# Attention and a two-layer network on one core: first q and k loaded in 1 KB packets, first products in two parts, and a new planned order

## The chip, the core and the metric

The kernel runs on one core of one Trainium2 chip. The core has five engines with a queue of their own each: TensorE (PE, matrix products), VectorE (DVE), ScalarE (ACT), GpSimd (POOL) and SyncE (SP, which only issues transfers here). They meet through semaphores. The metric is the device time of one launch in microseconds (us). Three runs of the kernel before gave 601.85, 602.19 and 604.92 us, so its median is 602.19 us.

## What is computed

Four sequences of 768 tokens with 8 heads of 64 numbers. A token attends to the first `n_global` (8) tokens and to itself and the 95 before it (`n_local` = 96), with a penalty that grows with distance. The result x (3072 tokens by 512) goes through a layer of 2048 units and back. All inputs are 32 bit floats, but the weights come as 64 bit floats and the two counts as 64 bit integers.

```python
scores = q @ k.T / sqrt(64) - slope[h] * dist        # kept where global or local, else -1e9
a = softmax(scores);  x = a @ v                      # x: 3072 x 512
h = x @ w_in                                         # 512 -> 2048
g = h * sigmoid(1.702 * h)
out = g @ w_out                                      # 2048 -> 512
```

## The kernel before

**Tiles.** Tokens are worked on in 24 blocks of 128 (`n`), and in 12 chunks `c` of two blocks each. The 2048 units are cut into 8 steps `s` of 256. The first four blocks (0 to 3) are the first block of each sequence; they need keys of their own block only, so the kernel starts with them (`prep_first`, `first`). The other 20 go through `prep` and `unit`, two heads at a time: scores `s` on PE (L536), a row maximum on DVE, the exponential and a split into a large and a small 16 bit part on ACT and DVE, a transposing transfer (`pt<-hl`), and the products with the values, `pv` (L567 to L569). `finish` divides by the sums, splits x into a large part `x_hi` and a small part `x_lo` and turns it (`xT`): by PE for blocks 0 to 3, by a transposing transfer for the others.

**Products.** A 32 bit product is made of three 16 bit ones: large by large, large by small, small by large. `up` (L787) makes h for chunks 0 to 2, in two halves (`fi`) of 12 products each; `up_two` (L827, tiles `pa`, `pb`) does it for chunks 3 to 11 with fewer products; `down` and `down_two` add into `y` (L895). `weights` makes the 16 bit weights out of the 64 bit words on DVE and ACT (`w`, `wa`, lines L370 to L378).

**The first four blocks.** `prep_first` loads q and k of a block into `raw`, 128 tokens on 128 partitions; a token's 64 numbers of one head are 256 bytes in a row, and such a packet is what a transfer moves at a time. PE turns two heads at once, a 128x128 block, into `tq` (L422, four turns for q and four for k); ACT and DVE bring the turned q into `QZ` and ACT the turned k into `KF` (its tile is shown as `hl`; L429). `first` then makes the scores (L604, in 32 bit, with a mask product L605), their maximum (`top`, L609), turns that (`aux`, L612), makes the scores again the other way round (`sT`, L623 to L625), takes the exponential (`pt`, L636) and multiplies by the values (`pv`, L631). `x` is made on DVE (L665 to L669), turned on PE (`tx`, L689), its large part is copied on ACT (L692) and the small part is made on DVE (L693). The masks `mm` depend on the two counts, which a transfer on ACT's queue brings to all 128 partitions (`ci`, L244); `counts`, `own` and `other` (L308 to L332) work them out on DVE.

**Order.** Nothing is ordered by hand. `Work.order` plans: each task has a price per engine and a due time, worked back from the tasks that wait for it, and each engine takes the ready task with the earliest due time. `NUDGE` shifts the due times of named groups (`up11` is chunk 1, step 1). Before 50 us the planner puts spare products (`spare`, L1056, tile `idle`, two of 128x512) where it finds PE without work for more than 0.5 us. What the engines do is that fixed order, each waiting for semaphores. Rings of buffers (`Ring`) hold the tiles; `tq`, `h`, `pa`, `pb`, `tx` of most blocks and `idle` share a ring of two PSUM banks (`r_h`). At the end the last `y` is scaled on ACT and written, and a flag that says whether the fast path held is read (L1066).

Of the kernel before, what the change touches and what calls it, by code (L numbers as in the profile page):

```python
# [19 lines left out]
P = 128  # L20
# [9 lines left out]
NUDGE = {"T2": -1.5, "down02": 1.4, "down05": -8.2, "down07": -0.8, "down103": 6.7, "down113": -5.5,  # L30
# [9 lines left out]
FIRST = 4  # L40
SIGN = [{"DVE": 0.62, "ACT": 1.0}]
TURN_X = 4
WARM, GAP = 50.0, 0.5
# [44 lines left out]
class Work:  # L88
# [15 lines left out]
    def order(self):  # L104
# [18 lines left out]
        for t in self.tasks:  # L123
            t.due += NUDGE.get(t.tag, 0.0)
        free = dict.fromkeys(("PE", "DVE", "ACT", "POOL", "SP"), 0.0)
# [4 lines left out]
        while len(done) < len(self.tasks) + spared:  # L130
            moved = False
            for e in free:
# [21 lines left out]
                if best is None:  # L154
                    if e != "PE" or now > WARM or now < worked + (GAP if worked > 7.0 else 0.0):
                        continue
                    best = self.spare(spared)
                    b = best.bufs[0]
                    if len(b.ring.taken) >= b.ring.bufs and (b.ring.taken[-b.ring.bufs].left or b.ring.taken[-b.ring.bufs].end > now):
                        continue  # L160
                    b.users, b.left = [best], 1
                    ready[best] = now
                    spared += 1
                t, us = best, best.on[e]
# [45 lines left out]
def kernel(  # L210
# [34 lines left out]
    cf = const.tile([P, 2, 2], F32, name="cf")  # L245
# [61 lines left out]
    def counts(e):  # L307
        nc.vector.tensor_copy(cf, ci)  # L308
        nc.vector.tensor_scalar(cnt, cf[:, :, 0], 0.0, None, ALU.is_lt)
        nc.vector.tensor_add(cnt, cnt, cf[:, :, 1])  # L310
        nc.vector.scalar_tensor_tensor(cnt, cnt, float(2 ** 32), cf[:, :, 0], ALU.mult, ALU.add)
# [29 lines left out]

    wk.tag = "masks"
    m0 = add({"POOL": 2.0}, places, bufs=[ints], want=-9.0)
    m0 = add({"DVE": 1.3}, distances, [m0], [ints, flt, mk], -4.0)
    late = add({"POOL": 1.0}, lambda e: None, [m0], want=0.0)
    m0 = add({"DVE": 0.65}, counts, [m0, late])
    covers = add({"DVE": 1.2}, covered, [m0])
    covers.soon = 300.0
    m1 = add({"DVE": 1.1}, own, [m0], [flt, mk])
# [49 lines left out]

    def guard(n, raw, ld, want):  # L400
# [7 lines left out]
    def prep_first(n):  # L408
# [6 lines left out]
        ld = load(n, raw, (0, 1))  # L415
        turned = []
        for z in range(2):
            tq = Buf(r_h, [P, NU, P], F32, f"tq{n}_{z}")

            def turn(e, z=z, tq=tq):  # L420
                for u in range(NU):
                    nc.tensor.transpose(tq()[:, u], raw()[:, z, 2 * u:2 * u + 2, :].rearrange("p h d -> p (h d)"), ident)  # L422

            turned.append((tq, add({"PE": 4 * TURN}, turn, ld[z:z + 1], [raw, tq])))

        def taken(to, z, part):
            tq, t1 = turned[z]
            return add({"ACT": 0.6, "DVE": 0.7}, lambda e: (
                nc.scalar.mul(to(), tq()[part], SX) if e == "ACT" else nc.vector.tensor_scalar(to(), tq()[part], SX, None, ALU.mult)),  # L429
                [t1], [tq, KF if z else QZ])  # L430

        rows = [slice(D * z, D * z + D) for z in range(2)]
        d["qk_ready"] = [zero, *(taken(lambda z=z: QZ()[rows[z], :, z, :], 0, rows[z]) for z in range(2)), taken(KF, 1, slice(0, P))]
# [85 lines left out]
    def unit(n, u, want_s, want_v):  # L519
# [29 lines left out]
        for j in range(2):  # L549
            t2 = add({"DVE": 0.365}, lambda e, j=j: rows(e, j), [t1, M2], [sp, pr])  # L550
# [30 lines left out]
    def first(n, want):  # L581
# [15 lines left out]
        for f in range(2):  # L597
# [9 lines left out]
            t1 = add({"PE": 4 * (mm_s + MM128)}, scores, [M1[f], *d["qk_ready"]], [sp, *QKs], want + 1.2 * f)  # L607
# [43 lines left out]
    xT, x_ready = {}, {}  # L651

    def finish(n):
# [30 lines left out]
        if n < TURN_X:  # L684
# [7 lines left out]
            t3 = add({"ACT": 0.5}, lambda e: nc.scalar.copy(xT[c]()[:, 0:NCC, t, :], tx()), [t2], [tx, xT[c]])  # L692
            x_ready[n] = add({"DVE": 0.61}, lambda e: nc.vector.tensor_sub(xT[c]()[:, NCC:, t, :], tx(), xT[c]()[:, 0:NCC, t, :]),  # L693
# [84 lines left out]
    def up(c, s, want):  # L778
# [11 lines left out]
        def hh():  # L790
            return ph().rearrange("p f t -> p (f t)")

        t1 = ups[c, s] = [add({"PE": 12 * MM256}, lambda e, fi=fi: mms(e, fi), [x_ready[2 * c], x_ready[2 * c + 1], W_ready[s, 0]],
                  [ph, xT[c], WT[s, 0]], want + 1.3 * fi) for fi in range(2)]
# [258 lines left out]
    def spare(n):  # L1053

        z = Buf(r_h, [P, 4 * P], F32, f"idle{n}")
        return Task({"PE": 2 * MM512 * (2 if n < 5 else 1)}, lambda e: [nc.tensor.matmul(z(), idle[:, 0:P], idle, start=True, stop=True)  # L1056
                                                  for _ in range(2)], (), [z], 0.0)
# [209 lines left out]
```

## Time and profile before

| what | value |
|---|---|
| median of three runs | 602.19 us |
| the profiled execution's own time | 602.55 us |
| its span in the profile | 600.8 us |
| busy: PE, DVE, ACT | 587.3, 502.9, 471.6 us |
| spare products (L1056) | 26 |

A span begins with the first instruction and ends with the last, and 1.75 us of the profiled execution's time lie around it. A row of the timeline gives start, duration, engine, line, tile, shape and count, and in brackets how long the engine was idle before it and what ended that. A PE record of a product lasts longer than the product holds up the next one: consecutive products overlap, so what one costs is read from one start to the next.

### The profile page before, as it was taken

The numbers are of one execution on the slowest core, as the hardware profiler recorded it, in microseconds if no ns is written. First come the engines' busy times: TensorE is split into PE (matmuls) and PEld (weight loads), VectorE is DVE, ScalarE is ACT, GpSimd is POOL, SyncE is SP. The second block draws the span as 40 slices with busy tenths as digits, with TensorE's granted clock in tenths as the row PEclk, the third lists the DMA queues.
The fourth block names the chain that finished last, engine by engine and source line by source line (L and its number), as shares of the span: only waits on it lengthen the run. The fifth ranks groups of instructions, "written<-read, shape, count | busy, mean of one in ns | idle before, by whom it ended". The sixth has DMA issues, their size and how long they took to land.

```text
span 600.8 us, 17038 instructions
## 1 busy us (share of the span) xinstructions
PE 587.3 (98%) x6816; PEld 445.8 (74%) x6816; DVE 502.9 (84%) x1177; ACT 471.6 (78%) x1098; POOL 5.8 (1%) x18
## 2 busy tenths in 40 slices
PE   8989999999999999999999999999999999999995
PEld 5878767776777867777677777777678778867895
DVE  6998999999999999789699789798979978766532
ACT  3878899978758988888688899788989988844432
POOL 3000000000000000000000000000000000000000
PEclk9999999999999999999999999999999999999998
DMA  8998898999976778969996999999989999910001
GB/s 221 316 249 254 235 251 191 196 187 203 198 139 127 160 117 182 199 141 206 194 222 153 227 204 233 206 229 198 240 181 227 227 205 237 231 29 3 36 2 40
DMA packets 268502, 109.58 MB, mean 182 GB/s; under 512 B 249536, under 2 KB 250048, under 8 KB 268416
## 3 DMA queue, kind: packets, MB, share of 16 engines
q1 hardware_dynamic: 268128, 108.43, 85.7%
q8 instruction: 55, 0.90, 0.6%
q14 instruction: 31, 0.25, 0.1%
q10 hardware_dynamic: 288, 0.00, 0.0%
HBM read 57.67 MB, written 6.29 MB: 106 GB/s over the span
## 4 chain that ended last, share of the span: by engine, by line
PE 82%; DMA 7%; ACT 4%; DVE 4%; issue 1%; SPq 1%; DVEq 0%; ACTq 0%
PE y L895 35%; PE pa L827 13%; PE h L787 10%; PE pb L827 10%; PE s L536 4%; DMA pt<-hl 2%; DMA out_dram<-yo 1%; PE s L604 1%; PE pv L567 1%; PE pv L568 1%; PE pv L569 1%; PE sT L623 1%; DMA raw<-in_k_dram 1%; DMA xT<-x 1%; DMA ws_00again<-in_moe_w_in_dram 1%
## 5 line engine op out<-in xcount | busy, mean ns | idle before, releaser
L895 PE MATMUL y<-w,g 128*128 128x512 f16 (+1 forms) x1248 | 266.9, 363 | 0.0
L895 PEld LDWEIGHTS <-g 128*128 128x128 f16 x1248 | 117.9, 98 | 103.3
L827 PEld LDWEIGHTS <-w 128*128 128x128 f16 x1728 | 101.2, 98 | 4.8
L552 ACT ACTIVATE p<-p,NM 128x232 f32<-128x232 f32 x160 | 76.5, 481 | 7.3 <-DVE NM L542 7.1
L827 PEld LDWEIGHTS <-T 128*128 128x128 f16 x1296 | 77.1, 98 | 6.2 <-issue 0.2
L787 PE MATMUL h<-xT,w 128*128 128x256 f16 x576 | 69.4, 273 | 0.5 <-DMA xT<-x 0.5
L542 DVE CUSTOM_DVE_ANT_0 p<-s,mm 128x232 f32<-128x232 f32 x160 | 57.7, 396 | 8.4 <-PE s L536 7.8
L787 PEld LDWEIGHTS <-w 128*128 128x128 f16 x576 | 55.2, 98 | 9.6 <-issue 0.8
L868 DVE SCALAR_TENSOR_TENSOR g<-t,g 128x512 f16<-128x512 f32 x72 | 49.3, 688 | 12.3 <-ACT g L867 12.0
L557 DVE TENSOR_TENSOR hl<-p,hl 128x464 f16<-128x464 f32 x80 | 50.9, 637 | 8.1 <-ACT hl L556 7.9
L867 ACT ACTIVATE g<-t 128x512 f16<-128x512 f32 x72 | 45.0, 628 | 9.5 <-DVE t L860 8.1
L859 ACT ACTIVATE t<-h 128x512 f32<-128x512 f32 (+1 forms) x72 | 35.9, 516 | 18.0 <-DVE h L835 14.9
L556 ACT CAST hl<-p 128x464 f16<-128x464 f32 x80 | 46.1, 577 | 4.2 <-DMA pt<-hl 2.3
L835 DVE TENSOR_TENSOR h<-pb,h 128x256 f32<-128x256 f32 x72 | 29.5, 420 | 22.6 <-PE pb L827 19.3
L827 PE MATMUL pa<-xS,T 128*128 128x128 f16 x648 | 45.0, 219 | 0.1
L860 DVE SCALAR_TENSOR_TENSOR t<-t,h 128x512 f32<-128x512 f32 (+1 forms) x72 | 38.3, 554 | 4.8 <-ACT t L859 4.2
L536 PEld LDWEIGHTS <-QK 128*128 128x128 f16 x640 | 36.4, 98 | 4.3 <-DMA QK<-QK 0.8
L536 PE MATMUL s<-QK 128*128 128x128 f16 x320 | 38.5, 219 | 0.6 <-DMA QK<-QK 0.6
L827 PE MATMUL pb<-xS,w 128*128 128x128 f16 x540 | 37.5, 219 | 0.0
L827 PE MATMUL pa<-xT,w 128*128 128x128 f16 x540 | 37.0, 219 | 0.0
L567 PE MATMUL pv<-VR,pt 128*128 128x64 f16 x288 | 34.8, 193 | 1.3 <-DMA pt<-hl 1.3
L569 PE MATMUL pv<-VR,pt 128*128 128x64 f16 x288 | 34.9, 193 | 0.0
(181 smaller groups left out, 1080.7 us busy)
## 6 DMA issues: line engine op xcount, KB each, us to landing
ws<-in_moe_w_in_dram SPq DMA_DIRECT2D x8, 1024.0 KB
ws<-in_moe_w_out_dram SPq DMA_DIRECT2D x8, 1024.0 KB
raw<-in_q_dram SPq DMA_DIRECT2D x24, 256.0 KB
raw<-in_k_dram SPq DMA_DIRECT2D x24, 256.0 KB
out_dram<-yo SPq DMA_DIRECT2D x22, 256.0 KB
QK<-QK SPq DMA_DIRECT2D x40, 128.0 KB
raw<-in_v_dram SPq DMA_DIRECT2D x20, 256.0 KB
ws_00again<-in_moe_w_in_dram SPq DMA_DIRECT2D x8, 512.0 KB
```

The lines of the kernel that those rows point to most:

```text
L536: nc.tensor.matmul(sp()[:, j, lo:hi], d["QK"]()[:, 0, h, :], K[:, 1 + z, h, P - (hi - lo):], start=(z == 0), stop=(z == 1), skip_group_che ...
L542: nc.vector.tensor_tensor_reduce(out=pr()[:, j, :], in0=sp()[:, j, :], in1=m, scale=-1.0 / SC, scalar=3.0e38, op0=ALU.add, op1=ALU.min, ac ...
L552: ex.append(add({"ACT": 0.473}, lambda e, j=j: nc.scalar.activation(pr()[:, j, :], pr()[:, j, :], AF.Exp, bias=NM[:, n, hs[j]:hs[j] + 1], ...
L556: t4 = add({"ACT": 0.5}, lambda e: nc.scalar.copy(hl()[:, 0, :, SKIP:], pr()), ex, [pr, hl])
L557: t5 = add({"DVE": 0.55}, lambda e: nc.vector.tensor_sub(hl()[:, 1, :, SKIP:], pr(), hl()[:, 0, :, SKIP:]), [t4], [pr, hl])
L567: nc.tensor.matmul(o, ph, V[:, 0, h], start=(s == 0), stop=False, skip_group_check=True)
L569: nc.tensor.matmul(o, pl, V[:, 0, h], start=False, stop=(s == ns - 1), skip_group_check=True)
L787: nc.tensor.matmul(ph()[:, fi, :], w1(s, cc, z, fi), X[:, y, cc, :], start=(j + cc == 0), stop=(j == 2 and cc == NCC - 1))
L827: nc.tensor.matmul(o()[:, fi], w, x()[:, y * NCC + 2 * k + cc, t], start=(first and fi + j + cc == 0), stop=(last and j + cc == 3), skip_g ...
L867: t4 = add({"ACT": 0.53}, lambda e, g=g, tt=tt: nc.scalar.mul(g()[:, 0], tt(), SG / (SX * SW)), u, [tt, g])
L868: t5 = add({"DVE": 0.61}, lambda e, g=g, tt=tt: nc.vector.scalar_tensor_tensor(g()[:, 1], tt(), SG / (SX * SW), g()[:, 0], ALU.mult, ALU.s ...
L895: nc.tensor.matmul(y(), part(zg, f), w2(s, z, f % 2)[:, m], start=(begin and f + j == 0), stop=(end and j == 2 and f == 2 * len(steps) - 1 ...
```

## The change

Four things are edited, and the planner makes a new order of the whole program out of them.

- **Loads of blocks 0 to 3** (`load_pairs`): a partition holds four consecutive tokens of one head (1 KB in a row), for two heads. Each of q and k comes in two transfers, where it was one. PE therefore turns 64 columns at a time: four turns as before into partitions 0 to 63 of `tq`, and four more products with the identity, in 32 bit and not in the turning mode, into partitions 64 to 127. The evictions read `tq` in a new order of columns; for blocks 0 and 1 that of k is cut in two halves (`KHALF`), and the first scores wait for the first half only.
- **Counts**: they go to one partition and are worked out there; one small product on PE (`pc`) with a row of ones brings them to all partitions. The second group of masks (`M2`) is made of four tasks on ACT alone; it was one on DVE or ACT.
- **First step's products** (`up`, s = 0, chunks 0 and 1): all 16 products with x's large part go first and wait only for the large part; the 8 with the small part follow and wait for it.
- **Spare products**: from the sixth on, one and not two. `HOLD` is empty and its code does nothing. `NUDGE` is another table.

```diff
-NUDGE = {"T2": -1.5, "down02": 1.4, "down05": -8.2, "down07": -0.8, "down103": 6.7, "down113": -5.5,
...
+NUDGE = {"T0": 4.2, "T1": 0.1, "T3": 0.6, "down01": -3.2, "down02": -4.7, "down03": -0.9, "down06": -32.8, "down07":
...
+KHALF = 2
...
+HOLD = {}
...
-    ci = const.tile([P, 2, 2], I32, name="ci")
+    ci = const.tile([1, 2, 2], I32, name="ci")
...
-        nc.scalar.dma_start(ci[:, j], src.bitcast(I32).rearrange("(o x) -> o x", o=1).broadcast_to([P, 2]))
+        nc.scalar.dma_start(ci[:, j], src.bitcast(I32).rearrange("(o x) -> o x", o=1))
...
+    pc = Buf(r_pv, [P, 2], F32, "pc")
+    m0 = add({"PE": 0.2}, lambda e: nc.tensor.matmul(pc(), row, c1, start=True, stop=True), [m0], [pc], COUNTS)
+    m0 = add({"DVE": 0.15}, lambda e: nc.vector.tensor_copy(cnt, pc()), [m0], [pc], COUNTS)
...
-    M2 = add({"DVE": 2.3, "ACT": 2.6}, lambda e: slopes(e, slice(0, 2)), [m2], [mk])
+    M2 = [add({"ACT": 0.65}, lambda e, f=f: slopes(e, slice(0, 2), range(2 * f, 2 * f + 2)), [m2], [mk]) for f in range(4)]
...
+    def load_pairs(n, raw):
+
+        b, i = place(n)
+        ld = []
+        for z in range(2):
+            src = (q, k)[z][b, :, i * P:(i + 1) * P, :].rearrange("(u e) (j t) d -> e u j (t d)", e=2, t=4)
+            dst = raw()[:, z].rearrange("p (e t) d -> p e (t d)", e=2)
+            ld.append([add({"SP": 0.45}, lambda e, src=src, dst=dst, o=o: nc.sync.dma_start(dst[:, o], src[o]), bufs=[raw]) for o in range(2)])
+        return ld
...
-                for u in range(NU):
-                    nc.tensor.transpose(tq()[:, u], raw()[:, z, 2 * u:2 * u + 2, :].rearrange("p h d -> p (h d)"), ident)
+                for u in range(4):
+                    nc.tensor.transpose(tq()[0:D, u], raw()[:, z, u, :], ident)
+                for u in range(4):
+                    nc.tensor.matmul(tq()[D:P, u], raw()[:, z, 4 + u, :], ident, start=True, stop=True, skip_group_check=True)
...
+        if s == 0 and c < 2:
+            large = add({"PE": 16 * MM256}, lambda e: [some(e, ((0, 0), (1, 0)), fi, fi == 0, False) for fi in range(2)],
+                        [x_large[2 * c], x_large[2 * c + 1], W_ready[s, 0]], [ph, xT[c], WT[s, 0]], want)
+            t1 = [add({"PE": 8 * MM256}, lambda e: [some(e, ((0, 1),), fi, False, True) for fi in range(2)],
+                      [large, x_ready[2 * c], x_ready[2 * c + 1]], [ph, xT[c], WT[s, 0]], want + 1.8)]
...
-        return Task({"PE": 2 * MM512 * (2 if n < 5 else 1)}, lambda e: [nc.tensor.matmul(z(), idle[:, 0:P], idle, start=True, stop=True)
-                                                  for _ in range(2)], (), [z], 0.0)
+        return Task({"PE": MM512 * (4 if n < 5 else 1)}, lambda e: [nc.tensor.matmul(z(), idle[:, 0:P], idle, start=True, stop=True)
+                                                                    for _ in range(2 if n < 5 else 1)], (), [z], 0.0)
```

How the order moves is seen at three places. The first is PE's queue behind the first eight spare products, at about 5 us. `tq0_0` is block 0's turned q, `tq0_1` its k, `tq1_0` block 1's q. Before:

```order
L422 MATMUL tq0_0_140<-ident_73,raw0_107 128x128 x3
L1056 LDWEIGHTS idle_71
L1056 MATMUL idle4_146<-idle_71 128x512 [waits PE_49]
L1056 LDWEIGHTS idle_71
L1056 MATMUL idle4_146<-idle_71 128x512
L422 MATMUL tq0_1_154<-ident_73,raw0_107 128x128 [waits DMAHW3_49,PE_49]
...
L422 MATMUL tq1_0_182<-ident_73,raw1_115 128x128 [waits DMAHW4_49,PE_49]
```

Of the change, the same place:

```order
L449 MATMUL tq0_0_155<-ident_76,raw0_95 64x128 x3
L451 MATMUL tq0_0_155<-ident_76,raw0_95 64x128 [waits DMAHW3_49]
L451 MATMUL tq0_0_155<-ident_76,raw0_95 64x128 x3
L362 MATMUL pc_168<-c1_68,row_69 128x2 [waits DVE_49]
L449 MATMUL tq0_1_170<-ident_76,raw0_95 64x128 [waits DMAHW4_49,PE_49]
L449 MATMUL tq0_1_170<-ident_76,raw0_95 64x128 x3
L451 MATMUL tq0_1_170<-ident_76,raw0_95 64x128 [waits DMAHW5_49]
L451 MATMUL tq0_1_170<-ident_76,raw0_95 64x128 x3
L449 MATMUL tq1_0_190<-ident_76,raw1_96 64x128 [waits DMAHW6_49,PE_49,Activation_49]
```

The spare products between the turns are gone, each turn has four more products (L451), `pc` stands between them, and `tq1_0`, which lies in the bank of `tq0_1`, now waits for ACT, where spare products used the banks in between. Of the 26 spare products 10 are left: these first eight and two before `sT` of block 0. All five spare tasks left are among the first five, which still hold two products.

The second place is ACT's queue at the start, with the evictions of the turned q and k of blocks 0 and 1 (k goes to `hl0` and `hl1`) and the masks `mm`. Before:

```order
L429 ACTIVATE QZ0_120<-tq0_0_140 64x4x128
L429 ACTIVATE hl0_89<-tq0_1_154 128x512
L338 ACTIVATE mm_91<-mk_126 128x128 x4
L429 ACTIVATE QZ1_133<-tq1_0_182 64x4x128
L429 ACTIVATE hl1_90<-tq1_1_218 128x512
L613 CAST mT0_79<-aux0_262 8x128
```

Of the change:

```order
L460 ACTIVATE hl0_92<-tq0_1_170 128x256 [waits PE_49]
L460 ACTIVATE hl0_92<-tq0_1_170 128x256
L351 ACTIVATE mm_94<-mk_135 128x128 [waits DVE_49]
L351 ACTIVATE mm_94<-mk_135 128x128 x3
L460 ACTIVATE QZ1_152<-tq1_0_190 64x4x128 [waits DVE_49]
L460 ACTIVATE hl1_93<-tq1_1_204 128x256 [waits PE_49]
L460 ACTIVATE hl1_93<-tq1_1_204 128x256
L351 ACTIVATE mm_94<-mk_135 128x256 x8
```

Each eviction of k is two instructions of half the size, and the eight wide masks, which DVE made before, stand on ACT ahead of the first weights.

The third place is PE's queue from the end of block 1's `sT` to the first `h`, at about 25 to 33 us. Before:

```order
L631 MATMUL pv1_374<-VF1_109,pt1_0_343 128x65 x4
L689 MATMUL tx0_383<-ident_73,x0_365 128x128 x4
L631 MATMUL pv1_374<-VF1_109,pt1_1_381 128x65 x3
L631 MATMUL aux1_304<-VF1_109,pt1_1_381 128x65
L1056 LDWEIGHTS idle_71
L1056 MATMUL idle11_400<-idle_71 128x512
...
L689 MATMUL tx1_415<-ident_73,x1_408 128x128 x4
L422 MATMUL tq2_0_421<-ident_73,raw2_336 128x128 x4
L422 MATMUL tq2_1_428<-ident_73,raw2_336 128x128 x4
L1056 LDWEIGHTS idle_71
L1056 MATMUL idle12_436<-idle_71 128x512
```

Of the change:

```order
L449 MATMUL tq2_0_394<-ident_76,raw2_97 64x128 x4
L451 MATMUL tq2_0_394<-ident_76,raw2_97 64x128 x4
L726 MATMUL tx0_406<-ident_76,x0_388 128x128 x4
L668 MATMUL pv1_413<-VF1_115,pt1_0_382 128x65 x4
L668 MATMUL pv1_413<-VF1_115,pt1_1_403 128x65 x3
L668 MATMUL aux1_332<-VF1_115,pt1_1_403 128x65
L449 MATMUL tq2_1_438<-ident_76,raw2_97 64x128 x4
L451 MATMUL tq2_1_438<-ident_76,raw2_97 64x128 x4
L726 MATMUL tx1_449<-ident_76,x1_435 128x128 x4
L449 MATMUL tq3_0_457<-ident_76,raw3_98 64x128 x4
L451 MATMUL tq3_0_457<-ident_76,raw3_98 64x128 x4
```

Three of the turns of blocks 2 and 3 stand where the spare products and waits were, ahead of the first `h`; before, the two of block 3 came behind it. `tq2_1` lies in the bank of `tq2_0`, and `tq3_1`, which follows the scores of block 2, in that of the first `h`. Behind 50 us the same tasks stand in another order; for one, between the last `pv` of block 5 and the first `h` of chunk 2 there were 4 groups of `s`, 3 of `y`, 2 of `h` and one of `pv`, and there are now 4, 4, 4 and one.

More of the change, by code (lines that the diff above doesn't have):

```diff
@@ L163, in order @@
                     spared += 1
+                if e in HOLD and best.due < 1e8:
+                    soon = [at for t, at in ready.items() if e in t.on and now < at <= now + min(HOLD[e], 0.5 * best.on[e]) and
+                            t.due < best.due - 1.0 and t.early() <= at]
+                    if now < held.setdefault((best, e), max(soon, default=0.0)):
+                        continue
                 t, us = best, best.on[e]
@@ L549, in unit @@
         for j in range(2):
-            t2 = add({"DVE": 0.365}, lambda e, j=j: rows(e, j), [t1, M2], [sp, pr])
+            t2 = add({"DVE": 0.365}, lambda e, j=j: rows(e, j), [t1, *M2], [sp, pr])
             checks.append(t2)
@@ L605, in scores @@
                     nc.tensor.matmul(sp()[:, j], id16, mm[:, h, 2], start=False, stop=True, skip_group_check=True)
-            t1 = add({"PE": 4 * (mm_s + MM128)}, scores, [M1[f], *d["qk_ready"]], [sp, *QKs], want + 1.2 * f)
+            t1 = add({"PE": 4 * (mm_s + MM128)}, scores, [M1[f], *(d["first_ready"][f] if n < FIRST else d["qk_ready"])], [sp, *QKs], want + 1.2 * f)
             d.setdefault("S", []).append(t1)
```

54 lines of the change are left out of this document (38 added, 16 removed), and 10 rows, old and new, of the table NUDGE.

## The prediction

> **What bounds the kernel now.** I read the busy shares first, then PE's busy time by stage, then what PE waited for.
>
> ```profile
> PE 587.3 (98%) x6816; PEld 445.8 (74%) x6816; DVE 502.9 (84%) x1177; ACT 471.6 (78%) x1098; POOL 5.8 (1%) x18
> ...
> 25.00:30.00 5.00, 4.27 (x35) 3.58 (x35) 4.54 (x11) 5.00 (x8) 0.00 (x0) 1.00 1.15 312
> 30.00:35.00 5.00, 4.09 (x36) 3.59 (x36) 4.83 (x8) 3.31 (x4) 0.00 (x0) 1.00 0.50 188
> 35.00:40.00 5.00, 3.80 (x33) 3.05 (x31) 4.83 (x7) 4.08 (x7) 0.00 (x0) 1.00 1.08 294
> 50.00:100.00 50.00, 50.00 (x405) 36.66 (x403) 46.07 (x84) 44.31 (x70) 0.00 (x0) 1.00 0.89 226
> ```
>
> The stages' columns are the stretch, its length, then the busy times of PE, PE's weight loads, DVE, ACT and POOL. PE is the bound: behind 50 us it has no gap for long stretches, and only the first 50 us leave it short of work. So the time is PE's products, plus PE's waits, plus a start and an end that the change doesn't touch. PE's waits, longest sum first (us in total, times, longest):
>
> ```profile
> PE idle L1056 <- ACT hl L429: 1.6, 2, 0.9
> PE idle L1056 <- POOL idle L252: 1.3, 1, 1.3
> PE pv L567 <- DMA pt<-hl: 1.3, 2, 0.8
> PE tx L689 <- DVE x L669: 0.7, 1, 0.7
> PE s L536 <- DMA QK<-QK: 0.6, 1, 0.6
> PE aux L612 <- DVE top L609: 0.6, 1, 0.6
> PE tq L422 <- DVE QZ L429: 0.6, 1, 0.6
> PE h L787 <- DMA xT<-x: 0.5, 1, 0.5
> PE tq L422 <- DMA raw<-in_k_dram: 0.2, 1, 0.2
> ```
>
> Beside the 1.3 us for the very first weights, which stay, six waits lie in the first steps (1.6+0.7+0.6+0.6+0.2 = 3.7 us) and four behind them (1.3+0.6+0.5 = 2.4 us, the `pv`, `s` and `h` rows). That is all a better order can win, together with the spare products.
>
> ```profile
> 15.68 0.27 PE L612 MATMUL aux<-ident,top 128*8 128x128 f32 x1
> 15.79 0.59 PE L1056 MATMUL idle<-idle 128*128 128x512 bf16 x2
> ```
>
> One allowance: a product's record runs past the start of the next one, here 0.27 us long with the next after 0.11. Idle time counts from the record's end, so each wait costs 0.16 us more than it shows: the six early ones 3.7+1.0 = **4.7 us**, the four later ones 2.4+0.6 = **3.0 us**.
>
> **The change part by part.** I sum against the profiled execution's own time, 602.55 us (span 600.8 and 1.75 around it), which is 0.36 over the median of 602.19.
>
> *Turning q and k.*
>
> ```profile
> 1.33 3.59 PE L1056 MATMUL idle<-idle 128*128 128x512 bf16 x8 [1.33 <-POOL idle L252]
> 4.74 1.09 PE L422 MATMUL tq<-ident,raw 128*128 128x128 f32 x4
> 5.61 1.06 PE L1056 MATMUL idle<-idle 128*128 128x512 bf16 x2
> 6.84 0.77 PE L422 MATMUL tq<-ident,raw 128*128 128x128 f32 x4 [0.17 <-DMA raw<-in_k_dram]
> 8.30 1.02 PE L1056 MATMUL idle<-idle 128*128 128x512 bf16 x4 [0.68 <-ACT hl L429]
> 9.16 0.60 PE L422 MATMUL tq<-ident,raw 128*128 128x128 f32 x4
> 9.59 0.59 PE L1056 MATMUL idle<-idle 128*128 128x512 bf16 x2
> 10.03 0.38 PE L604 MATMUL s<-hl,QZ 128*128 128x128 f32 x2
> 10.25 0.22 PE L605 MATMUL s<-mm,id 128*128 128x128 bf16 x1
> 10.30 0.44 PE L604 MATMUL s<-hl,QZ 128*128 128x128 f32 x2
> 10.58 0.22 PE L605 MATMUL s<-mm,id 128*128 128x128 bf16 x1
> ...
> 25.03 1.00 PE L631 MATMUL pv<-VF,pt 128*128 128x65 f32 x8
> 25.87 0.61 PE L689 MATMUL tx<-ident,x 128*128 128x128 f32 x4
> ```
>
> Four turns take 9.59 - 9.16 = 0.43 us, 0.11 each; their number stays, 32. A 32 bit product in two passes takes 10.25 - 10.03 = 0.22 us. The 32 new products with the identity have this shape but for 64 columns of weights, which no row shows at that width. Bounds: 0.21 us, from `pv` (8 passes in 25.87 - 25.03 = 0.84), and 0.28, the second score product (10.30 to 10.58). I take 0.22, the one that follows 32 bit work as these will: 32 x 0.22 = **+7.0 us** (6.7 to 9.0). All of it lies on PE, which has nothing to hide it beyond waits and spare products. `pc` adds 0.1.
>
> *Spare products.* Sixteen of 26 go. At 8.30 four take 9.16 - 8.30 = 0.86, 0.215 each; the two at 5.61, like the first eight ((4.74 - 1.33)/8 = 0.43), ran at half that speed. 14 x 0.215 + 2 x 0.43 = **-3.9 us**. That later spare tasks hold one product changes nothing: none is planned beyond the fifth.
>
> *Half speed at the start.* The clock column says 1.00 all along, yet products take twice as long until about 7.2 us (0.43 against 0.215). The first four turns have that in both kernels; the four products behind them, now at 5.6 us, get it too: 8 passes x 0.11 = **+0.8 us** (0 to 1.5).
>
> *Early waits.* The six, 4.7 us, go with their places: the turns and `pv` that fill them are the added work. New ones I work out from the order. `tq1_0` waits for both halves of `hl0`:
>
> ```profile
> 7.65 0.60 ACT L429 ACTIVATE hl<-tq 128x512 f32<-128x512 f32 x1 [1.20 <-PE tq L422]
> 9.24 0.91 ACT L338 ACTIVATE mm<-mk 128x128 bf16<-128x128 f32 x4 [0.99 <-DVE mk L327]
> ...
> L843 ACT COPY h<-pa 128x256 f32<-128x256 f32 x36 | 13.1, 364 | 10.1 <-PE pa L827 9.9
> ```
>
> PE ends `tq0_0` at 4.74+0.87+1.7 = 7.3 and `tq0_1` at 8.7; ACT starts 0.2 later and needs two pieces of 0.36 (the group with 256 columns), to 9.6: 0.9 us for PE. At 30 us `tq2_1` waits for the second half of block 2's `QZ`, which stands behind a weight step on ACT, and `tq3_1` for the DVE step that frees h's bank; I put them at 0.8 and 0.5, about the longest waits of that kind there now (0.9 for ACT, 0.6 for DVE in the rows of waits). Together **+2.2 us** (0 to 4.5, the lower end if ACT and DVE run ahead, the upper about the early waits of before).
>
> *The 1 KB packets and the counts.* q's four turns follow the eight spare products without a gap (4.74), so q came in time and its earlier landing wins nothing; k's wins the 0.2 us counted above. The counts reach one partition, and their four DVE steps now stand ahead of the first `QZ`. ACT had its first masks done at 9.24+0.91 = 10.2; with `tq0_0` ready 1.5 us later (7.3 for 4.74+1.09) they come by 11.7 at most, and PE, at 9.6 + 2 x 1.3 for block 1's turns, reaches the first scores at 12.2. So neither is late, by half a us; beyond that each us of slip would be a us. The evictions read PSUM with a stride, which no row shows: I take their old durations, 0.6 us; nothing less is likely, twice as long would add about 0.4 us to the wait of `tq1_0`. The eight masks moved to ACT (8 x 0.36 = 2.9 us) lie beside 16 score products of 0.33 each (0.28 to the start of the mask product, at 10.58, and 0.05 for that), 5.3 us of PE. The first `h` starts without the small part, but at 33 us it comes behind five further turns, by when DVE, on my count, has that part too: nothing (down to -0.6, the one DVE step that it skips).
>
> Sum of the first steps: 7.0 + 0.1 - 3.9 + 0.8 - 4.7 + 2.2 = **+1.5 us**.
>
> *The order behind 50 us.* The products are the same, so only waits count. Transfers took:
>
> ```profile
> 126.37 1.31 PE h L787 x12
> 128.03 0.41 PE s L536 x8
> 128.44 1.29 PE y L895 x6
> 131.96 4.97 DMA xT<-x
> 289.29 6.21 DMA pt<-hl
> 344.08 4.54 DMA QK<-QK
> 403.17 6.29 DMA pt<-hl
> 410.03 0.67 PE pa L827 x12
> ```
>
> For `xT` PE had 4 groups of `s`, 3 of `y`, 2 of `h` and a `pv` (0.35) to do meanwhile, 1.6+3.9+2.6+0.35 = 8.5 us; now 4, 4, 4 and one, 12.4. For the first `pv` of block 14 (289 us): 6 groups of `pa`/`pb`, 2 of `y`, 3 of `s`, 7.8 us; now 7, 4 and 2, 10.7. For that of block 19 (403 us): 4, 4, 2, 8.7; now 7, 4, 3, 11.1. These three waits were 0.5+1.3 and 3 x 0.16, 2.3 us, and each gets over twice what it lacked, so I drop them. The one for `QK` (0.8) I keep, and 0.6 for one new wait of that size, since every group has moved. **-1.7 us** (-3.0, all gone, to +2.0, two or three more).
>
> The end is as before: the last four groups of `y`, one eviction, one transfer. Total 602.55 + 1.5 - 1.7 = **602.4 us**.
>
> **The rivals.** *Faster: the order covers everything.* If ACT and DVE are early enough, the 2.2 us of new early waits and the last 1.3 us later on fall away: 602.4 - 2.2 - 1.3 = 598.9 us. For it: DVE and ACT are under 90% busy over the whole span. Against it: between 25 and 40 us DVE is 91 to 97% busy, the very place of two of the three waits. Chance 0.22.
>
> *Slower: the half-width turns.* Every turn now goes to 64 columns of the array, then to the other 64, and back to full width: 24 changes. If the array had to run empty at each (the 0.16 us of a record's overhang), 24 x 0.16 = 3.9 us, 606.3 in all. If turns in 32 bit lost their short form at this width, 32 x (0.22 - 0.11) = 3.5 us, 605.9. It decides from 0.13 us a change, or 0.1 us a turn. The row at 15.68 speaks against both: `aux` is a 32 bit turn with 8 columns and takes 0.11 us to the next start, with no gap ahead or behind; but it writes the array's first columns, and no row shows the second 64. Chance 0.13. The Trainium skill, TensorEngine Tiling (Array Packing), states in Key Properties that a change of tiling mode drains TensorE, and in Restrictions and Gotchas that column tiling excludes the transpose mode for FP32 input. By the first rule the sum would be 606.3, by the second 605.9; the `aux` row, 0.11 us, agrees with neither.
>
> *Slower: new waits behind 50 us*, two or three transfers of 5 to 6 us that now have too little work in front; 3.5 us more than I count gives 605.9. Chance 0.07.
>
> *The change doesn't do what it says*: the single spare products never occur, and the 1 KB packets move work that wasn't late. Both are in the forecast, as is the added PE work that eats the gain.
>
> **How the numbers follow.** Forecast 0.58 around 602.4, faster 0.22 at 598.9, slower 0.20 (0.13+0.07) near 606. About 0.5%, 3 us, is what a measurement of this kernel can tell from no change. The forecast's own range, 599.6 to 605.2, holds the bounds of the single terms taken together; reaching to the two sides until no more than 2 in 10 is left out gives 598.6 to 606.2.
>
> **What would show it.** Right: PE shows about 10 spare products, 32 new ones at 0.22 us, `tq1_0` idle for close to 1 us at 9 us on ACT, the first scores at about 12 us; later on no wait at `xT` of chunk 2 or at blocks 14 and 19. Wrong: turns over 1.4 us a tile, gaps around them, first scores before 11 us, or more than 3 us of idle PE behind 60 us. A different rate of the array in the first 7 us would shift the start by up to 1 us either way.

## The result and the profile after

The changed kernel takes 619.06 us (median of three runs, 617.89 to 620.42) against 602.19: a ratio of 1.0261, 95% interval 1.023 to 1.0292. The forecast was no change, 602.4 us, in a range up to 606.2. The profiled execution took 617.89 us with a span of 615.8, so 15.0 us of span are to be explained.

The busy shares of the changed kernel and its stages, with the columns of before (some early stretches are added):

```profile
PE 598.0 (97%) x6866; PEld 454.8 (74%) x6866; DVE 502.0 (82%) x1171; ACT 473.8 (77%) x1108; POOL 5.8 (1%) x18
...
5.00:10.00 5.00, 3.08 (x22) 2.35 (x23) 1.80 (x7) 0.59 (x1) 1.56 (x3) 1.00 0.27 94
10.00:15.00 5.00, 2.34 (x19) 1.62 (x18) 2.41 (x10) 1.74 (x7) 0.00 (x0) 1.00 1.08 268
15.00:20.00 5.00, 4.25 (x20) 3.50 (x21) 1.04 (x2) 1.96 (x7) 0.00 (x0) 0.54 0.56 136
25.00:30.00 5.00, 5.00 (x50) 4.70 (x49) 4.36 (x7) 2.67 (x4) 0.00 (x0) 1.00 0.74 211
...
45.00:50.00 5.00, 2.00 (x10) 1.57 (x10) 3.35 (x5) 1.47 (x2) 0.00 (x0) 0.61 0.91 281
```

Read the last three columns: granted clock, DMA share, GB/s. Between 5 and 10 us the DMA engines are busy a quarter of the time, just when PE has little to do. At 15 and at 45 us the clock falls to about half. At 25 us, where PE lacked work before (4.27 of 5 us), it is full now, being late by then. PE has 10.7 us more busy time than before (598.0 for 587.3); 32 new products less 16 spare ones make only 7.0 - 3.9 = 3.1 of that.

What PE waited for, in the changed kernel (total, times, longest), without the one for the very first weights:

```profile
PE h L835 <- DVE xT L731: 3.9, 1, 3.9
PE tq L451 <- DMA raw<-in_q_dram: 1.6, 2, 0.9
PE tq L451 <- DMA raw<-in_k_dram: 1.5, 2, 0.8
...
PE tq L449 <- DMA raw<-in_k_dram: 1.0, 1, 1.0
PE pv L604 <- DMA pt<-hl: 0.9, 2, 0.5
PE pa L879 <- ACT h L895: 0.8, 1, 0.8
PE tq L449 <- ACT hl L460: 0.7, 1, 0.7
PE tq L449 <- ACT QZ L460: 0.5, 1, 0.5
PE tq L449 <- DMA raw<-in_q_dram: 0.4, 1, 0.4
PE s L573 <- DMA QK<-QK: 0.2, 1, 0.2
```

Six waits for the loads of q and k (1.6+1.5+1.0+0.4 = 4.5 us) were not there before, where these rows came to 0.2 us. The longest wait is for a step of DVE. PE's timeline at the start:

```profile
5.30 0.60 PE L449 MATMUL tq<-ident,raw 128*64 128x128 f32 x4 [0.38 <-DMA raw<-in_q_dram]
6.64 1.09 PE L451 MATMUL tq<-ident,raw 128*64 128x128 f32 x8 [0.74 <-DMA raw<-in_q_dram]
...
14.98 0.62 PE L449 MATMUL tq<-ident,raw 128*64 128x128 f32 x4 [1.02 <-DMA raw<-in_k_dram]
16.35 1.97 PE L451 MATMUL tq<-ident,raw 128*64 128x128 f32 x8 [0.76 <-DMA raw<-in_k_dram]
18.25 0.80 PE L641 MATMUL s<-hl,QZ 128*128 128x128 f32 x2
```

Six of the eight halves of the first four tiles wait for a transfer of their own (a half is the turns of L449 or the products of L451), the last eight passes run at half speed (1.97 for 1.09 us), and the first scores start at 18.25 us. Before it was 10.03; the prediction said 12.2.

### The profile page after: what moved, and what is told of

It reads as the page before. It is cut to its first block, busy times and chain, and to the rows that moved or that the text cites. A ratio compares the mean times of both kernels' runs of the same rounds, so it can differ in the third digit from the quotient of the medians.

```text
span 615.8 us, 17165 instructions
## 1 busy us (share of the span) xinstructions
PE 598.0 (97%) x6866; PEld 454.8 (74%) x6866; DVE 502.0 (82%) x1171; ACT 473.8 (77%) x1108; POOL 5.8 (1%) x18
## 4 chain that ended last, share of the span: by engine, by line
PE 88%; DMA 7%; ACT 2%; SPq 1%; DVE 1%; issue 0%; DVEq 0%; ACTq 0%
PE y L947 38%; PE pa L879 14%; PE pb L879 10%; PE h L825 9%; PE s L573 5%; DMA ws<-in_moe_w_in_dram 2%; PE s L641 2%; DMA pt<-hl 2%; DMA raw<-in_k_dram 2%; PE pv L604 1%; PE sT L660 1%; PE pv L606 1%; PE pv L605 1%; DMA ws_11again<-in_moe_w_out_dram 1%; SPq L424 1%; PE pv L668 1%
## 5 line engine op out<-in xcount | busy, mean ns | idle before, releaser
L879 PEld LDWEIGHTS <-w 128*128 128x128 f16 x1728 | 101.7, 98 | 6.6 <-issue 1.0
L825 PE MATMUL h<-xT,w 128*128 128x256 f16 x528 | 63.9, 273 | 0.0
L825 PEld LDWEIGHTS <-w 128*128 128x128 f16 x528 | 50.5, 98 | 7.8
```

What stands on the lines that cost most here:

```text
L825: nc.tensor.matmul(ph()[:, fi, :], w1(s, cc, z, fi), X[:, y, cc, :], start=(j + cc == 0), stop=(j == 2 and cc == NCC - 1))
L879: nc.tensor.matmul(o()[:, fi], w, x()[:, y * NCC + 2 * k + cc, t], start=(first and fi + j + cc == 0), stop=(last and j + cc == 3), skip_g ...
```

## The experiments

**The theory** (A in the expectations). The pattern of `load_pairs` has DRAM's address run over four pairs of heads first (`u`, outermost), then 32 groups of tokens. With 4 entries there, a transfer keeps only 4 of the 16 DMA engines busy; the eight transfers of the first two blocks, and later the eight of blocks 2 and 3, then take far longer than they did. The DMA share of 0.27 (4.3 of 16) is the hint. **The rivals**: B, two transfers to a tensor and 1 KB packets cost something by themselves; C, the added products and the new order do.

**How many entries stand outermost.** Three kernels change only that, from 4 to 32, 8 and 2. In e1_spread (32):

```diff
-            src = (q, k)[z][b, :, i * P:(i + 1) * P, :].rearrange("(u e) (j t) d -> e u j (t d)", e=2, t=4)
+            src = (q, k)[z][b, :, i * P:(i + 1) * P, :].rearrange("(u e) (j t) d -> e j u (t d)", e=2, t=4)
...
-            src = lambda: tq()[part].rearrange("p t (u j) -> p u j t", u=NU)[:, u]
+            src = lambda: tq()[part].rearrange("p t (j u) -> p u j t", u=NU)[:, u]
```

In e2_eight, and then in e4_two, the same line becomes (these two load other heads and tokens than they should, in as many packets of the same size):

```diff
+            src = [(q, k)[z][b, :, 64 * o:64 * o + 64, :].rearrange("h (j t) d -> h j (t d)", t=4) for o in range(2)]
...
+            src = [(q, k)[z][b, 2 * o:2 * o + 2, 0:256, :].rearrange("h (j t) d -> h j (t d)", t=4) for o in range(2)]
```

> Edit: the two loads of each first q and k address DRAM with 32 groups of four tokens as the outermost dimension, in place of the four pairs of heads; still 128 packets of 1 KB each, and the evictions read PSUM in the new order. Nothing else changes. Theory A (each of these loads runs on 4 of the 16 DMA engines, because the outermost dimension of its DRAM pattern has 4 entries, so it takes about 1.4 us, eight of them in a row end near 16 us, and PE waits, drops its clock and stays behind): the loads take under 0.6 us each, the DMA share between 2 and 8 us rises from 0.27 to over 0.8, the first scores start near 12 us in place of 18, the clock stays full at 15 to 22 us, and the time is 602.4 us (599 to 606), which is what the prediction's sum gives without the failed step. Rival B (two transfers to a tensor or packets of 1 KB have a fixed cost, or SP issues them too slowly): loads still over 1.2 us, 615 to 620 us. Rival C (the added products and the new order cost the 17 us by themselves): loads faster but 613 us or more.

> Edit: the same loads with 8 entries in the outermost dimension of the DRAM pattern in place of 4 (all eight heads of 64 tokens in one load); so the q and k of the first four blocks hold other heads and tokens than they should, with the same number, size and packets of the transfers and the same work behind them. Theory A: a load runs on 8 DMA engines and takes about 0.7 us, the DMA share between 2 and 8 us is near 0.5, and the time is 604 to 609 us. Rival B (a fixed cost of two transfers to a tensor or of 1 KB packets): loads still about 1.4 us and 615 to 620 us. Rival C (added products and order): 613 us or more with faster loads.

> Edit: the same loads with 2 entries in the outermost dimension of the DRAM pattern in place of 4 (two heads of 256 tokens in one load); again the q and k of the first four blocks hold other heads and tokens, with the same number and size of packets. Theory A: a load runs on 2 DMA engines and takes about 2.8 us, the DMA share between 2 and 8 us is near 0.13, the last of the first eight ends near 25 us in place of 16, and the time rises by 9 us and more over that of the change, 627 to 640 us. Rivals B and C: no difference from the change, 615 to 620 us.

Measured: 605.44 us with 32 (ratio to before 1.0041, 1.0023 to 1.0058), 605.67 with 8, 619.06 with 4 (the change), 639.11 with 2 (one run each for 8 and 2; before beside them took 602.9). The stretch from 4 to 6 us shows the cause, since hardly anything but these loads runs there. With 2, 4, 8 and 32 entries outermost:

```profile
4.00:6.00 2.00, 0.93 (x3) 0.02 (x1) 0.95 (x4) 0.00 (x0) 1.85 (x4) 1.00 0.13 47
```

```profile
4.00:6.00 2.00, 1.52 (x7) 0.38 (x5) 1.18 (x4) 0.00 (x0) 1.85 (x4) 1.00 0.27 96
```

```profile
4.00:6.00 2.00, 2.00 (x9) 1.02 (x8) 0.71 (x3) 0.00 (x0) 1.85 (x4) 1.00 0.49 141
```

```profile
4.00:6.00 2.00, 2.00 (x15) 1.33 (x13) 0.71 (x3) 0.00 (x0) 1.85 (x4) 1.00 0.68 196
```

The same stretch of before, with packets of 256 B and tokens outermost:

```profile
4.00:6.00 2.00, 2.00 (x8) 1.01 (x7) 0.00 (x0) 0.14 (x1) 1.85 (x4) 1.00 0.88 193
```

The DMA share goes 0.13, 0.27, 0.49 (2.1, 4.3 and 7.8 of 16 engines) and the rate 47, 96, 141 GB/s: the share doubles with the entries, for packets of the same number and size. A single 1 KB packet of these loads took 46 ns in all four kernels (median of the trace's packet records of the first 9 us), and with 2, 4 and 8 entries there were most often 2, 4 and 8 of them under way at a time: a packet isn't slower, fewer run side by side. Rivals B and C expected nothing of this and are out as the main cause. With 32 entries the share is 0.68, where the expectation said over 0.8, and 8 entries do as well in the end; another limit is near then. SP's issue of the loads of e1_spread (shortest, median and longest, in ns):

```profile
L424 SPq DMA_DIRECT2D raw<-in_q_dram x8: 535/598/711, 0.8 to 17.5; - x8
```

128 KB each 0.6 us is 218 GB/s, close to the 196 seen, and SP issues the first eight without a gap, from 0.75 to 5.98 us: these loads come at SP's pace.

The Trainium skill, DMA: Bandwidth & Descriptors, section "Why a DMA increments its semaphore by 16 and not by 1", states the rule: a transfer uses the largest number of engines up to 16 that divides the outermost dimension of both its patterns. The shares for 2, 4 and 8 entries agree with 2, 4 and 8 engines; the 0.68 for 32 doesn't contradict 16, since SP's pace is the limit there.

**Which loads cost what.** The spread pattern for blocks 0 and 1 alone, and for blocks 2 and 3 alone.

In e6_first_two (e7_last_two has `n >= 2`; the evictions follow):

```diff
-            src = (q, k)[z][b, :, i * P:(i + 1) * P, :].rearrange("(u e) (j t) d -> e u j (t d)", e=2, t=4)
+            src = (q, k)[z][b, :, i * P:(i + 1) * P, :].rearrange("(u e) (j t) d -> e j u (t d)" if n < 2 else "(u e) (j t) d -> e u j (t d)", e=2, t=4)
```

> Edit: the loads of e1_spread (32 groups outermost) for blocks 0 and 1 alone; those of blocks 2 and 3, near 20 us, stay as the change has them, with 4 entries outermost. It splits the 13.6 us between the change and e1_spread by place. Theory A: the first scores start near 12 us, the clock stays full at 15 to 22 us, but the eight transfers of blocks 2 and 3 still take about 1.4 us each one after another, so the weights behind them land late, DVE stands in a weight step in front of the step that takes x's large part away, and the first h still waits about 4 us for it with a stretch of half clock behind: 610 to 613 us. If the late weights come only from the late start: 604 to 607 us. If the start costs nothing because later work has slack: 616 to 620 us.

> Edit: the loads of e1_spread for blocks 2 and 3 alone; those of blocks 0 and 1 stay as the change has them. Theory A: first scores still near 18 us with the clock at half from 15 to 22 us, but no wait of 4 us of the first h and no second stretch of half clock: 611 to 615 us, and with e6_first_two the two gains add up to the 13.6 us between the change and e1_spread within 2 us. If the late start alone makes the weights late: 616 to 620 us.

Measured: 612.13 us (1.0152, 1.0102 to 1.0202) and 613.64 (1.0174, 1.0132 to 1.0216). Counted from before beside each, the change stands at +16.9, e6 at +9.5, e7 at +11.0, e1 at +2.5: the first two blocks give back 7.4 us, the last two 5.9, together 13.3 of the 14.4. Both places are real, and within the intervals, about 3 us to either side for e6 and e7, they add.

How blocks 2 and 3 reach PE is seen in four views of the changed kernel: SP's queue, the chain of waits, DVE's and PE's timeline.

```profile
28.58 5.46 SPq L424 DMA_DIRECT2D raw<-in_k_dram  x2
34.15 2.71 SPq L216 DMA_DIRECT2D ws<-in_moe_w_in_dram  x1
```

```profile
34.15 12.48 DMA ws<-in_moe_w_in_dram
```

```profile
46.65 0.69 DVE L390 TENSOR_SCALAR w<-ws 128x1024 int32<-128x1024 int32 x1 [5.49 <-DMA ws<-in_moe_w_in_dram]
47.26 0.68 DVE L731 TENSOR_TENSOR xT<-tx,xT 128x512 f16<-128x512 f32 x1
```

```profile
48.00 1.87 PE L835 MATMUL h<-xT,w 128*128 128x256 f16 x8 [3.88 <-DVE xT L731]
```

The weights are issued on SP behind the pair loads, the last of which hold it for 5.46 us, and land 12.48 us later. DVE stands 5.49 us in the weight step L390, behind it in DVE's queue stands the step that makes x's small part (L731), and PE waits 3.88 us for that. In e6_first_two it is the same row 6 us earlier, with PE's wait in the second fence:

```profile
40.60 0.70 DVE L390 TENSOR_SCALAR w<-ws 128x1024 int32<-128x1024 int32 x1 [5.49 <-DMA ws<-in_moe_w_in_dram]
```

```profile
PE h L835 <- DVE xT L731: 4.7, 1, 4.7
```

In e7_last_two and e1_spread PE's list of waits has no such row.

**The half clock.** Spare products in the pauses of three early turns, the loads left slow.

```diff
+                if n < 2 and (n or z):
+                    for _ in range(4):
+                        nc.tensor.matmul(tq().rearrange("p u t -> p (u t)"), idle[:, 0:P], idle, start=True, stop=True)
                 for u in range(4):
                     nc.tensor.transpose(tq()[0:D, u], raw()[:, z, u, :], ident)
```

> Edit: the loads stay slow, but twelve spare products are put ahead of three of the early turns (four each, 0.215 us apiece), where PE idles for the loads anyway. It asks whether the half clock at 15 to 22 us is a cost of its own that comes from PE's pauses. If so: full clock there and about 2 us gained, 615 to 617.5 us. If the clock follows something else, such as the time or the DMA: half clock at the same place, 618 to 621 us, the spare products adding up to 1 us where they outlast the loads.

Measured: 618.45 us (1.0253, 1.0209 to 1.0296), which is the change's own ratio. But the first half clock did go; the stages of e3_warm, and two of its waits:

```profile
15.00:20.00 5.00, 4.27 (x36) 3.60 (x34) 0.98 (x3) 2.88 (x9) 0.00 (x0) 1.00 0.59 142
...
40.00:45.00 5.00, 5.00 (x30) 3.83 (x29) 1.36 (x2) 1.77 (x3) 0.00 (x0) 0.66 1.05 305
45.00:50.00 5.00, 1.69 (x10) 1.10 (x8) 2.91 (x4) 1.36 (x1) 0.00 (x0) 0.76 0.88 275
```

```profile
PE h L838 <- DVE xT L734: 3.3, 1, 3.3
PE tx L729 <- DVE x L709: 1.9, 1, 1.9
```

and DVE's wait for the weights of the second matrix (tile `ws`), in the changed kernel and in e3_warm:

```profile
DMA ws<-in_moe_w_out_dram: 0.8, 1
```

```profile
DMA ws<-in_moe_w_out_dram: 3.5, 1
```

So the pauses had halved the clock, as expected; the 2 us that this should have won were not there, and neither expectation was met in full. PE was ahead by 2.6 us at its first `tx` (33.1 us for 35.7) and lost it all by its first `h` (42.3 for 42.2): 1.9 us to DVE's x, and 0.7 to another stretch of half clock from 40.7 us on, where eight passes ahead of that `h` took 1.84 us for 1.09. DVE in turn stood 2.7 us longer for the weights. While the loads are slow, they and not PE set that point.

**The rest of the change without the added products.** Old packets of 256 B and old full-width turns, in the change's order (e5_old_loads); then with one transfer to a tensor in place of two, once with a task and price of its own, by which the planner makes a new order (e9), and once in e5's order (e10). First e5 against the change, then the load's line in e9 and in e10.

```diff
-            src = (q, k)[z][b, :, i * P:(i + 1) * P, :].rearrange("(u e) (j t) d -> e u j (t d)", e=2, t=4)
-            dst = raw()[:, z].rearrange("p (e t) d -> p e (t d)", e=2)
-            ld.append([add({"SP": 0.45}, lambda e, src=src, dst=dst, o=o: nc.sync.dma_start(dst[:, o], src[o]), bufs=[raw]) for o in range(2)])
+            src = (q, k)[z][b, :, i * P:(i + 1) * P, :].rearrange("h p d -> p h d")
+            dst = raw()[:, z]
+            ld.append([add({"SP": 0.45}, lambda e, src=src, dst=dst, o=o: nc.sync.dma_start(dst[:, 4 * o:4 * o + 4], src[:, 4 * o:4 * o + 4]), bufs=[raw]) for o in range(2)])
...
-                for u in range(4):
-                    nc.tensor.transpose(tq()[0:D, u], raw()[:, z, u, :], ident)
-                for u in range(4):
-                    nc.tensor.matmul(tq()[D:P, u], raw()[:, z, 4 + u, :], ident, start=True, stop=True, skip_group_check=True)
+                for u in range(NU):
+                    nc.tensor.transpose(tq()[:, u], raw()[:, z, 2 * u:2 * u + 2, :].rearrange("p h d -> p (h d)"), ident)
```

```diff
+            ld.append([add({"SP": 0.9}, lambda e, src=src, dst=dst: nc.sync.dma_start(dst, src), bufs=[raw])])
...
+            ld.append([add({"SP": 0.45}, lambda e, src=src, dst=dst, o=o: nc.sync.dma_start(dst, src) if o == 0 else None, bufs=[raw]) for o in range(2)])
```

> Edit: q and k of the first blocks come in packets of 256 B as before (still two transfers each, of four heads), are turned by four full-width transposes as before and evicted without a stride, which takes the 32 added products out; the planner's prices are left alone, so the order, the spare products, the split first step and the counts are those of the change. Theory A: the loads are spread over 16 engines and q and k come in time, and PE has 32 x 0.22 = 7 us less to do, of which some becomes waiting: 597 to 602 us. Rival B as far as it lies in two transfers to a tensor, and rival C as far as it lies in the order: 610 us or more. If C lies in the added products alone: 600 us here, and e1_spread stays above 610.

> Edit: as e5_old_loads, with each q and k in one transfer in place of two, priced at 0.9 us on SP's queue. It asks whether the two transfers of a tensor are worth anything once they are spread. If the first half landing earlier is what wins: 600.5 to 602 us, slower than e5_old_loads by 1 us and more, for k lands later. If not: 598.5 to 600.5 us, the same as e5_old_loads within 1 us.

> Edit: the order of e5_old_loads to the row on every engine, with each of the first q and k in one transfer of all eight heads in place of two of four. In e9_old_loads_one the planner was given other tasks on SP's queue and changed the order of every engine, so its 5 us say nothing of the transfers alone. If it was the order: 598.5 to 600.5 us here, the same as e5_old_loads. If one transfer for two costs time by itself: 603 to 605 us as there.

Measured: 599.55 us (0.9941, 0.9921 to 0.9961), 604.52 (1.0052, 1.0026 to 1.0077) and 598.59 (0.9922, 0.99 to 0.9943). Two transfers or one is the same in the same order. e9's expectation failed: its 5 us are the order alone, since e10 has e9's transfers in e5's order. Against before, both e5 and e10 are a little faster (0.6 and 0.8%): the change's other parts win 3.4 to 4.3 us together, the 16 spare products less among them, and e10 beats both kernels.

> Edit: e5_old_loads with the planner's price of a turn put back to four transposes, so that it no longer reckons with products that are not there; the order of every engine changes for it, the work doesn't. If a right price is worth anything by itself: 598 to 600 us. If the table of due times fits one order alone, and any other order loses waits that it had avoided, as e9_old_loads_one did: 602 to 606 us.

e8 is e5 with one price (`4 * TURN` for `4 * TURN + 4 * FP128`) and so another order: 601.47 us (0.9978, 0.9963 to 0.9993), between its two expectations. A right price alone doesn't pay.

**The size of two terms.** The 32 added products twice over, in e1_spread; and sixteen spare products put back into e10.

```diff
-                for u in range(4):
+                for u in (0, 0, 1, 1, 2, 2, 3, 3):
                     nc.tensor.matmul(tq()[D:P, u], raw()[:, z, 4 + u, :], ident, start=True, stop=True, skip_group_check=True)
```

```diff
+                if (n, z) in ((1, 0), (2, 0), (2, 1), (3, 0)):
+                    for _ in range(4):
+                        nc.tensor.matmul(tq().rearrange("p u t -> p (u t)"), idle[:, 0:P], idle, start=True, stop=True)
                 for u in range(NU):
```

> Edit: e1_spread with each of the 32 added products of q and k with the identity run twice, the second writing the same values again; the order is otherwise that of e1_spread to the row. It measures what 32 such products cost in their place. By the prediction's 0.22 us each, all on PE's path: 605.4 + 7.0 = 612.4 us (611 to 614). If part of them lies in waits, as the 5.9 us between e1_spread and e5_old_loads hint: 609 to 611 us.

> Edit: e10_one_same_order with sixteen spare products of the kind that the change took out put back, four each ahead of the turns of tq1_0, tq2_0, tq2_1 and tq3_0 (the places of before aren't in this order); the order is otherwise that of e10_one_same_order to the row. It prices the term of -3.9 us for spare products. If all sixteen lie on PE's path: 598.6 + 16 x 0.215 = 602.0 us (601 to 603). If PE waits at those places anyway, as the traces of e10_one_same_order show for tq1_0 and tq2_1 (0.75 and 0.59 us): 599.5 to 601 us. If work behind them has slack as well: 598 to 599.5 us.

Measured: 610.97 us (1.0145, 1.012 to 1.0171) for e11, 5.5 over e1_spread; 601.59 (0.9968, 0.9946 to 0.999) for e12, 3.0 over e10. The spare products of e12 write the turn's own bank, so they stand behind the waits that they were to fill, and e12 says nothing on filling. PE's waits in e1_spread and then in e11, without the one for the very first weights:

```profile
PE pa L879 <- ACT h L895: 1.4, 2, 0.8
...
PE pv L604 <- DMA pt<-hl: 0.9, 1, 0.9
PE tq L449 <- ACT hl L460: 0.7, 1, 0.7
PE tq L449 <- ACT QZ L460: 0.5, 1, 0.5
PE s L573 <- DMA QK<-QK: 0.5, 1, 0.5
PE pv L604 <- DMA VR<-VG: 0.3, 1, 0.3
```

```profile
PE tq L449 <- ACT hl L460: 0.7, 1, 0.7
PE tq L449 <- ACT QZ L460: 0.5, 1, 0.5
PE pb L879 <- ACT h L884: 0.4, 1, 0.4
```

The traces show why 7.0 us of products cost less. In the profiled execution of e11, 2.7 us of waits far behind the start are gone; that PE comes later there, and so finds the other engines and transfers ready, is the likely reason. Four waits fewer save 4 x 0.16 more: 7.0 - 2.7 - 0.6 = 3.7, and the two spans differ by 3.8 (607.0 and 603.2). The sum is good to about 0.7 us, since e11 was also 0.65 us later through its first four turns (5.71 us for 5.06). The medians differ by 5.5, so part of the saving varies from one execution to the next.

## Why the prediction was wrong

**The step that failed** is "The 1 KB packets and the counts". It said that q "came in time and its earlier landing wins nothing", and held that neither q nor the masks were late. It took the new transfers to be at least as quick as the old ones and gave them no price. The edit was in the diff, `"(u e) (j t) d -> e u j (t d)"`, but its outermost 4 was not read as a number of engines. The step's own fallback was right: "beyond that each us of slip would be a us". The first scores slipped from 12.2 to 18.25 us, and mending that alone gave back 7.4; the first half clock went with it (granted clock 1.00 from 15 to 20 us in e6_first_two). No term looked past the first scores, where the loads of blocks 2 and 3 lost 5.9 more through the weights behind them on the same queue. The profile of the changed kernel adds up against e1_spread: 7.2 us more waiting (11.5 for 4.3, the first weights left out) and 5.6 us more busy time for the same products (598.0 for 592.4), which is the half clock above all, make 12.8, and their spans differ by 12.6.

**With the loads mended** the rest of the sum can be read. For e1_spread the sum gives its 602.4, no change; measured is 2.5 us above before. Rows of PE's timeline of e1_spread, at the start and at 32 us:

```profile
8.78 0.62 PE L449 MATMUL tq<-ident,raw 128*64 128x128 f32 x4 [0.75 <-ACT hl L460]
...
10.35 0.62 PE L449 MATMUL tq<-ident,raw 128*64 128x128 f32 x4
10.91 1.09 PE L451 MATMUL tq<-ident,raw 128*64 128x128 f32 x8
11.93 0.49 PE L641 MATMUL s<-hl,QZ 128*128 128x128 f32 x2
...
31.92 0.66 PE L726 MATMUL tx<-ident,x 128*128 128x128 f32 x4
32.41 0.60 PE L449 MATMUL tq<-ident,raw 128*64 128x128 f32 x4
```

and one row of e11, where sixteen passes stand in place of eight:

```profile
8.47 1.96 PE L451 MATMUL tq<-ident,raw 128*64 128x128 f32 x16
```

- *New products, +7.0.* Right: eight more passes make e11's row longer by 0.87 us, 0.22 a product, and all of it is on PE. The waits that it covers later on were not foreseen.
- *Half-width turns, a rival with a chance of 0.13.* Its first mechanism holds. Four turns and four products take 11.93 - 10.35 = 1.58 us, not 0.43 + 0.88 = 1.31, and 1.4 was the bound given for "wrong". The 0.27 lies at two changes, the one to the second half of the columns and the one away from it, about the 0.13 each from which the rival was said to decide. The step from full width to the first half is free: at 32.41 us the first turn of `tq` starts 0.11 us after the last of `tx`. So 16 of the 24 changes cost something, +2.2 us over eight tiles, where the rival had 3.9. The second, turns that lose their short form, didn't come: the four take 10.91 - 10.35 = 0.56 us with a change in it. The `aux` row was poor evidence, as the prediction half saw: it uses the first columns only. The Trainium skill, TensorEngine Tiling (Array Packing), Key Properties, says that a change of tiling mode drains TensorE, and that a change of tile alone does not. The two changes at the second half agree, at 0.13 us, if the first half still counts as full width; the free step at 32.41 fits that, but no run shows the mode.
- *Spare products, -3.9.* Ten are left, as said. Sixteen cost 3.0 us in e12, a little less than 16 x 0.215.
- *Half speed, +0.8.* Not there in this execution: e1_spread's first four turns took 0.53 us (4.53 to 5.06), full speed already. In e11 the same four took 0.99 (4.72 to 5.71). When the full speed begins differs from one execution to the next, so this term was luck either way, as the prediction's last sentence allowed.
- *Early waits, -4.7 and +2.2.* The six of before went. Of the three new ones `tq1_0` took 0.75 (0.9 said), one for `QZ` 0.5 (0.8), the third didn't appear. First scores at 11.93, 12.2 said.
- *Behind 50 us, -1.7.* Half wrong. The waits at `xT` of chunk 2 and at block 19 went, but block 14's (484 products of `pv` behind 50 us stand ahead of it in each kernel) stayed, 0.9 us in e1_spread. SP's queue there:

```profile
290.44 0.38 SPq L961 DMA_DIRECT2D out_dram<-yo  x1
290.90 1.51 SPq L595 DMA_TRANSPOSE pt<-hl  x1
```

  The transposing transfer is issued at 290.90, right behind another. What it moves was ready at 289.43, but SP was at other transfers until 290.82, so PE's work since the scores was no measure of its lead. New waits for ACT came at `pa` (1.4 us).

In spans, e1_spread against before: 7.0 + 0.1 + 2.2 - 3.9, 1.8 less waiting (4.3 for 6.1) and three waits fewer (0.5) give +3.1; it is +2.4. Most of the rest is the earlier full speed: e1_spread was through its first four turns at 5.06 us, before at 5.61. So the forecast of the rest was fair and its range held it, though misses cancelled in part, which is luck. The changes at the second half cost 2.2 us and the waits behind 50 us 2.5 us more than the sum had (1.4+0.9+0.5+0.3 and five times 0.16, where it had 0.8+0.6); the half speed cost about 1.2 and the early waits about 0.7 less. The loads alone took the time out of the range.

Left open: the split of the first step and the counts were not tried alone, since the planner reorders everything for such an edit, and what an order is worth by itself is as large (5.9 us between e9 and e10).

## What to carry to other kernels

For each transfer that is rewritten, read the outermost dimension of both patterns before packet sizes: 1 KB packets over 4 engines moved 96 GB/s where 256 B packets over more had moved 193. Then look at what is queued behind it, on SP and on the engines that wait, since here the weights behind slow loads came late, and that cost 5.9 us beside the 7.4 of the first loads. Where a planner makes the order, compare an edit at a fixed order; otherwise the order's own few us are taken for the edit's.

## What the runs showed of the hardware

- The share of the DMA engines that a load kept busy doubled with its outermost DRAM dimension: 0.13, 0.27 and 0.49 for 2, 4 and 8 entries, 47, 96 and 141 GB/s, at the same 46 ns for a packet of 1 KB. With 32 entries SP's 0.6 us of issue for each transfer was the limit, near 196.
- The clock fell to half at 15.4 us, for 6.8 us by the changed kernel's clock records, although PE had not paused over 1.02 us since its first turns; it had been busy 3.08 and 2.34 us of the two 5 us stretches ahead. Twelve short spare products kept that away.
- A change to the second 64 columns of the array and one away from them cost about 0.13 us each, and the step from full width to the first 64 nothing (starts 0.11 us apart at 32.41 us in e1_spread); a 32 bit turn in the first 64 columns took the same 0.11 us as at full width.
